# Thresholded attention and a GELU layer pair on one core: moving the weights' conversion within the first batch, and zeroing less of the V tiles

## The chip, the cores and the metric

The kernel runs on one core of one Trainium2 chip. The metric is the device time of one execution in microseconds (us); the median of several runs is compared. Five engines work side by side, each through its own instructions in order, and wait for one another by semaphores: TensorE (PE; its weight loads are shown apart as PEld), VectorE (DVE), ScalarE (ACT), GpSimd (POOL) and SyncE (SP, which here only issues transfers).

## The reference

```python
scores = scale * q @ k.T                       # per batch and head, S x S
thresh = max(scores, axis=-1) - tau
scores = where(scores >= thresh, scores, -1e9)
attn = exp(scores - max(scores)); attn = attn / (sum(attn) + 1e-9)
x = (attn @ v)  ->  (B*S, H*D)                 # 4608 x 512
h = x @ w_in                                   # 512 x 2048
g = 0.5 * h * (1 + erf(h / sqrt(2)))
out = g @ w_out                                # 2048 x 512
```

There are 8 batches, 8 heads, 576 tokens and a head size of 64. Queries, keys and values are 32-bit floats. The two weight matrices come as 64-bit floats, because a 32-bit array was multiplied by a 64-bit scalar when they were made. The kernel turns each weight into a 32-bit float by integer arithmetic on its two halves. This is the conversion that the change moves.

## The kernel before

**Pairs, chunks and slots.** Heads are handled in pairs (`p`, 32 pairs, 4 to a batch, `HP = 4`). The 576 query rows of a pair are cut into five chunks: four of 128 rows for both heads (`i` = 0 to 3) and one (`i` = 4, `NC`) that holds the 64 last rows of both heads. The main loop (L1065) goes over slots `n`, one pair and one chunk each. In the first batch (`BATCH` = 20 slots) the order is special: first chunks 0 and 1 of all four pairs (n = 0 to 7), then chunks 2, 3 and 4 of each pair in turn (n = 8 to 19). So n = 10, 13, 16 and 19 are the short chunks.

**One slot.** `scores` (L403) puts the products of a chunk into two PSUM tiles `sc`, one for each head of the pair. There are just two such buffers, so the scores of the next slot wait until the last reader of these is done. `softmax_head` takes the row maximum on VectorE (L415), the threshold on GpSimd (L416) and the exponential on ScalarE (L418). `softmax_tail` zeroes what lies under the threshold and sums the rows, in one VectorE instruction for each head (L435), which is that last reader. In the first batch, TensorE turns the result in the slot after (`turn_p_early`, L349), with copies on ScalarE (L356, L365); `weigh_v` multiplies it with the values (L538), and `divide_early` (L457 to L465) divides by the sums. For the first slots of the first pairs, queries and keys are turned on TensorE too (`turn_qk_early`, L319 to L336).

**The first layer beside the attention.** When 256 tokens have all their heads, a block of the two matrix layers can start. `fill` (L638) puts products of the first layer (L614) and of the second (L629) between the attention's products, by a budget of time that the list `GOAL` sets. In the first batch it starts at slot 10 and does the first half of block 0; a product is placed only when its weight pieces have been converted.

**Conversion of the weights.** There are 32 pieces of 128x512 weights, 16 of each matrix, 512 KB each as 64-bit floats. `load_piece` (L183) brings a piece into a free place of `xall` or `turned_p`. `conversions` (L186) is a generator that issues the steps of one piece after another: two ScalarE instructions (L202 for the high half's power, L203 for the low half), two VectorE instructions on the piece before (L210, L212), then the load of another piece. `add_low_bits` (L222) adds the two parts on GpSimd (L226) in a later slot. `convert(ns)` is called at the end of every slot. It adds `ns` to a debt and takes steps until the VectorE time that they stand for, 340 + 720 = 1060 ns a piece, has paid it. All engines work through their instructions in order, so what `convert` puts at the end of a slot stands before the maximum, the exponential and the later work of the next slot.

**The V tiles.** Four tiles `v_sb` of 128 x 2 x 5 x 64 hold the values of a pair. For the first four pairs, `load_v_early` fills chunks 0 to 3 of both heads in all partitions, and of the last chunk (index `NC` = 4) only 64 partitions for each head; the other 64 must be zero, because the short chunks of both heads are multiplied in one go. The tiles are zeroed once at the start, on VectorE, before the first scores (L1027, L1028).

Of the kernel before, what the change touches and what calls it, by code (L numbers as in the profile page):

```python
# [18 lines left out]
def kernel(  # L19
# [35 lines left out]
    HP = H // 2  # L55
    NP = B * HP
    EARLY = HP
    NC = S // P
# [66 lines left out]
    q_tail = [att.tile([P, P], FP32, name=f"q_tail{i}") for i in range(4)]  # L125
    v_sb = [att.tile([P, 2, KR, D], FP32, name=f"v{i}") for i in range(4)]
# [59 lines left out]
    def conversions():  # L186

        vec = nc.vector
        ahead = []
        done = 0
        while raws or ahead:
            if raws:
                dst, raw, slot = raws.pop(0)
                lo, hi = (raw.rearrange("p (f w) -> p f w", w=2)[:, :, i] for i in range(2))  # L200
                power = gp.tile([P, PIECE], U32, tag="g", name="power")
                nc.scalar.activation(power.bitcast(FP32), hi.bitcast(FP32), AF.Copy, bias=0.0, scale=2.0 ** -112)  # L202
                nc.scalar.activation(dst.bitcast(U32), lo, AF.Copy, bias=0.0, scale=2.0 ** -29)  # L203
                ahead.append((dst, hi, power, slot))
                yield 0
            if len(ahead) == LATER and done == len(pieces) - LATER:
                yield None
            if len(ahead) == 2 or not raws:
                dst, hi, power, slot = ahead.pop(0)
                vec.tensor_scalar(power, power, 3, 0x7FFFFFF8, op0=ALU.logical_shift_left, op1=ALU.bitwise_and)  # L210
                yield 340
                vec.scalar_tensor_tensor(power, hi, 0x80000000, power, op0=ALU.bitwise_and, op1=ALU.bitwise_or)  # L212
                x_free.extend(slot)
                yield 720
                sums_due.append((dst.bitcast(U32), power))
                load_piece()
                done += 1
                yield 0
# [3 lines left out]
    def add_low_bits(most=len(pieces)):  # L222

        for _ in range(min(most, len(sums_due))):
            dst, power = sums_due.pop(0)
            nc.gpsimd.tensor_tensor(dst, power, dst, op=ALU.add)  # L226
            converted[0] += 1
# [3 lines left out]
    def convert(ns, least=0):  # L231

        if conv["steps"] is None:
            conv["steps"] = conversions()
        conv["debt"] += ns
        while conv["debt"] > 0 or least > 0:
            took = next(conv["steps"], None)
            if took is None:
                return
            conv["debt"] -= took  # L240
            least -= took
# [31 lines left out]
    def load_early(p):  # L273
        b, hp = divmod(p, HP)
        s = st[p] = {}
        for name, src in (("q", q), ("k", k)):

            if p == 2:
                at = s[name + "_slot"] = x_slot()
                t = x_rows(at)[:, 0:2 * (NC + 1) * D].rearrange("p (e c d) -> p e c d", e=2, d=D)  # L280
            else:
                t = ld.tile([P, 2, NC + 1, D], FP32, tag=name, name=name)
            s[name] = t
            eng = (nc.scalar, nc.gpsimd)[p] if p < 2 and name == "k" else nc.sync
            for e in range(2):
                rows = src[b, 2 * hp + e, 0:MAIN, :]
                if name == "q":
                    eng.dma_start(t[:, e, 0:NC, :].rearrange("p (g c) d -> p g (c d)", c=2),
                                  rows.rearrange("(g p c) d -> p g (c d)", p=P, c=2))
                else:  # L290
                    eng.dma_start(t[:, e, 0:NC, :], rows.rearrange("(p t) d -> p t d", p=P))
            eng.dma_start(t[0:TAIL, :, NC, :], src[b, 2 * hp:2 * hp + 2, MAIN:S, :].rearrange("e s d -> s e d"))
# [101 lines left out]
    def scores(p, i):  # L394
        s = st[p]
        n = 1 if i == NC else 2
        sc = s["sc", i] = [ps.tile([P, 2, 512], FP32, tag="sc", name="sc", bufs=2) for _ in range(n)]
        for h in range(2):
            for e in range(n):
                rows = slice(0, P) if i == NC else slice(e * D, (e + 1) * D)  # L400
                lhsT = s["q_tail"] if i == NC else s["qT"][rows, i * P:(i + 1) * P]
                at = h * HALF + (TAIL if p < EARLY and e == 0 else 0)
                nc.tensor.matmul(  # L403
                    sc[e][:, h, 0:HALF], lhsT=lhsT, rhs=s["kT"][rows, at:at + HALF], start=True, stop=True)
# [36 lines left out]
    def invert(p, i):  # L441

        den = st[p]["sum", i]
        nc.vector.reciprocal(den, den)
# [579 lines left out]
    for _ in range(2):  # L1024
        load_piece(nc.gpsimd)
    load_early(2)
    for t in q_tail + v_sb:  # L1027
        nc.vector.memset(t, 0.0)  # L1028
    turn_qk_early(0)
    conv["steps"] = conversions()  # L1030
# [10 lines left out]
    BATCH = HP * SLOTS  # L1041
# [23 lines left out]
    for n in range(len(slots) + WEIGH + 1):  # L1065
        p, i = slots[n] if n < len(slots) else divmod(n, SLOTS)
        early = p < EARLY
        last = slots[n - 1] if 0 < n <= len(slots) else None
        if p < NP:
            scores(p, i)  # L1070
            softmax_head(p, i)
            add_low_bits()
            if last and last[0] < EARLY:
                invert(*last)
            if p < HP - 1 and i == 0:
                turn_qk_early(p + 1)
        elif n == len(slots):
            early_end.close()
            weights_first()
        gelus(0)  # L1080
        if n == BATCH:
            gelus_held()
        table()
        for args in due:
            weigh_v(*args)
            divide_early(*args)
        due = []
        if p > EARLY and i == WEIGH:
            for lo, hi in (0, WIDE), (WIDE, S):
                weigh_v(p - 1, lo, hi)  # L1090
            if p == NP:
                divide(p - 1)
        owed += (goal(n) - goal(n - 1)) * BLK_NS * (PARTS[i] if not early and p < NP else 1.0)
        if early:
            fill(owed, tokens)
            owed = 0.0
            table()
        if last and last[0] < EARLY and last[1] < NC:
            turn_p_early(*last)
        if p < NP:  # L1100
            softmax_tail(p, i)
        if p < NP and not early:
            turn_p(p, i)
        if p < NP and not early:
            if i == 2:
                regroup(p, 1)
            if i > 2:
                regroup(p, i)
            if i == NC:
                divisors(p)  # L1110
        if last and last[0] < EARLY and last[1] == NC:
            turn_p_early(*last)
        if p < 2 and i == 0:
            for _ in range(2):
                load_piece()
            load_v_early(p + 2)
        if p == 1 and i == NC:
            load(HP)
        if n == BATCH - 3:
            load(HP + 1)  # L1120
        if n == BATCH:
            for t in pd_tail + [turned_p[:, e, h, :, :] for e in range(2) for h in range(2)]:
                nc.gpsimd.memset(t[:, NB:4 * KR, :], 0.0)
        if EARLY < p < NP and i == DIVIDE:
            divide(p - 1)
        if p >= HP and i == 1 and p + 2 < NP:
            loads = load_steps(p + 2)
        if p >= HP:
            next(loads, None)
        if p >= HP and i == 1 and p + 1 < NP or p == HP - 1 and i == 2:  # L1130
            scale_q(p + 1)
        if p >= HP - 1 and i == 2 and p + 1 < NP:
            turn_qk(p + 1)
        convert(0 if n == 0 else 1200 if n < 3 else 1900 if n < BATCH - 1 else 1e9)
        if not early:
            lag[0] = 2 if p < NP else 0
            if n != BATCH:
                fill(owed, tokens)
                owed = 0.0
        if last and last[0] < EARLY:  # L1140
            if last[1] == 1:
                due.append((last[0], 0, TOK))
            if last[1] == NC:
                due.append((last[0], TOK, S))
        if n == START - 1:
            tokens = TOK
        elif n == BATCH + 1:
            tokens = S
        elif p > EARLY and i == DIVIDE and p % HP == 0 or p == NP and i == WEIGH:
            tokens = p // HP * S  # L1150
            leaving += [n for n in AWAY if n in x_blk and (n + 1) * TOK <= tokens]
        elif leaving and i < 2:
            put_away(leaving.pop(0))
# [35 lines left out]
```

## Time and profile before

| what | value |
|---|---|
| median of 3 runs | 1350.75 us (1350.1 to 1352.02) |
| profiled span | 1351.2 us, 19824 instructions |
| busy: TensorE, VectorE, ScalarE, GpSimd | 98%, 77%, 45%, 49% |
| granted TensorE clock, mean | 0.989 |
| slot 0, slot 10, slot 18 open (first row maximum) | 11.32, 70.88, 124.27 us |
| zeroing of the four V tiles | 2.61 us of VectorE, from 6.12 |
| L210, L212 (VectorE, one piece) | 0.42 and 0.69 us, when nothing is in the way |
| L226 (GpSimd, one piece) | 1.26 us |

The profile is that of one execution. A group line names source line, engine, operation and tiles; the bracket at the end gives the idle time of the engine just before, and what ended it ("<-DVE p L435": VectorE's instruction of line 435 that wrote p; "issue": nothing that the profile shows). The clock column is the share of the full TensorE clock that was granted in a stretch. A busy TensorE is not a TensorE at its peak: the ends of matmuls are modelled, and a stretch at half clock is as busy as one at full clock.

### The profile page before, as it was taken

The page shows a single profiled execution, that of the slowest core. Times are in us where ns is not written, and L with a number is a line of the kernel's source. Part 1 is how long each engine was busy: PE and PEld are TensorE (multiplying, and loading weights), DVE is VectorE, ACT ScalarE, POOL GpSimd, SP SyncE. Part 2 cuts the span into 40 slices and gives each one's busy share as a digit, 9 for nine tenths or more (in the row PEclk, how much of TensorE's full clock was granted, in tenths as well). Part 3 has the DMA queues.
Part 4 walks back from the last instruction along what each step waited for, and adds up shares of the span by engine and source line. Part 5 has one row for each costly group of instructions (what it writes and reads, how often), then busy time and mean ns, then how long its engine had stood idle before and what let it go on. Part 6 is the DMA issues. An engine that isn't in the chain of part 4 may idle for free.

```text
span 1351.2 us, 19824 instructions
## 1 busy us (share of the span) xinstructions
PE 1326.1 (98%) x6282; PEld 895.3 (66%) x6282; DVE 1043.9 (77%) x2005; ACT 605.6 (45%) x1027; POOL 657.2 (49%) x1091
## 2 busy tenths in 40 slices
PE   8899899999999999999999999999999999999998
PEld 6577457467467467457557557568787787877877
DVE  6877687788888888878888888874758698385775
ACT  7877437438447538437638536413201112211120
POOL 4766444555655565554554551144363513635530
PEclk8899899999999999999999999999999999999999
DMA  8743276677778687787688677500000031000003
GB/s 258 188 137 76 67 168 147 149 169 182 159 179 176 159 202 168 162 207 167 153 210 181 150 180 150 117 8 0 1 0 1 16 110 32 0 1 0 1 0 78
DMA packets 209782, 152.40 MB, mean 113 GB/s; under 512 B 113360, under 2 KB 193088, under 8 KB 209680
## 3 DMA queue, kind: packets, MB, share of 16 engines
q1 hardware_dynamic: 187648, 110.43, 37.1%
q0 software_dynamic: 21312, 39.37, 10.5%
q10 hardware_dynamic: 720, 1.34, 0.3%
q8 instruction: 51, 0.84, 0.3%
q14 instruction: 51, 0.42, 0.1%
HBM read 55.97 MB, written 12.52 MB: 51 GB/s over the span
## 4 chain that ended last, share of the span: by engine, by line
PE 93%; ACT 2%; DMA 2%; DVE 1%; issue 1%; POOL 0%; SPq 0%; DVEq 0%; ACTq 0%; POOLq 0%
PE bank L802 34%; PE o_ps L629 17%; PE hT L614 16%; PE sc L403 14%; PE xT L538 11%; DMA x<-xall 1%; DMA q<-in_q_dram 1%; ACT p L418 1%; PE tr L349 1%; DVE nmx L415 1%; ACT pT L356 0%; DVE p L435 0%; PE tr L457 0%; ACT power L202 0%; DVE power L212 0%
## 5 line engine op out<-in xcount | busy, mean ns | idle before, releaser
L418 ACT ACTIVATE p<-sc,nmx 128x576 f32<-128x576 f32 x288 | 201.9, 739 | 278.7 <-DVE nmx L415 278.5
L435 DVE SCALAR_TENSOR_TENSOR p<-sc,thr,p 128x576 f32<-128x576 f32 x288 | 226.2, 816 | 77.9 <-ACT p L418 71.4
L416 POOL TENSOR_SCALAR thr<-nmx,tau_eff 128x1 f32<-128x1 f32 x288 | 85.3, 296 | 369.0 <-DVE nmx L415 359.4
L415 DVE TENSOR_REDUCE nmx<-sc 128x1 f32<-128x576 f32 x288 | 205.4, 750 | 53.4 <-PE sc L403 52.1
L614 PE MATMUL hT<-xall,w_in 128*128 128x256 f32 x1024 | 243.0, 387 | 0.0
L629 PE MATMUL o_ps<-w_out,g 128*128 128x512 f32 x512 | 238.4, 606 | 0.0
L614 PEld LDWEIGHTS hT<-xall,w_in 128*128 128x128 f32 x1024 | 190.4, 191 | 50.5 <-issue 23.0
L684 DVE TENSOR_TENSOR c<-c,bank 128x320 f32<-128x320 f32 x304 | 147.2, 488 | 33.7 <-PE bank L802 20.5
L684 DVE TENSOR_TENSOR o<-o,bank 128x256 f32<-128x256 f32 x240 | 99.8, 420 | 93.7 <-PE bank L802 88.7
L403 PE MATMUL sc<-kT,qT 64*128 64x288 f32 x960 | 161.8, 434 | 9.8 <-DVE p L435 9.1
L538 PE MATMUL xT<-pT,v 128*64 128x256 f32 (+1 forms) x1280 | 168.0, 416 | 0.1
L629 PEld LDWEIGHTS o_ps<-w_out,g 128*128 128x128 f32 x512 | 93.7, 191 | 110.2 <-issue 107.6
L499 DVE STREAM_TRANSPOSE turned_p<-p 128x1152 f32<-128x1152 f32 x112 | 154.4, 1378 | 3.9
L403 PEld LDWEIGHTS sc<-kT,qT 64*128 64x128 f32 x960 | 92.2, 188 | 83.4 <-issue 69.5
L538 PEld LDWEIGHTS xT<-pT,v 128*64 128x64 f32 x1280 | 91.4, 140 | 75.3 <-issue 14.6
L802 PE MATMUL bank<-w_out,c 128*128 128x256 f32 x480 | 120.2, 381 | 0.5 <-DVE o L684 0.5
L269 POOL DMA_DIRECT2D v<-in_v_dram x208 | 111.3, 538 | 3.7 <-issue 1.3
L802 PEld LDWEIGHTS bank<-w_out,c 128*128 128x128 f32 x480 | 89.9, 190 | 18.8 <-DVE o L684 3.0
L855 ACT ACTIVATE c<-c 128x320 f32<-128x320 f32 (+1 forms) x80 | 46.9, 623 | 114.6 <-DVE c L684 114.5
L684 POOL TENSOR_TENSOR c<-c,g 128x320 f32<-128x320 f32 (+1 forms) x40 | 50.6, 1273 | 67.4 <-DVE c L684 67.4
L802 PE MATMUL bank<-t_out,c 128*128 128x256 f32 x320 | 82.7, 381 | 0.0
L802 PE MATMUL bank<-t_out,g 128*128 128x256 f32 x320 | 82.1, 379 | 0.0
(179 smaller groups left out, 1771.8 us busy)
## 6 DMA issues: line engine op xcount, KB each, us to landing
pT<-turned_p SPq DMA_DIRECT2D x448, 160.0 KB, 3.6
pT<-pd_tail SPq DMA_DIRECT2D x112, 80.0 KB, 3.0
q<-in_q_dram POOLq DMA_DIRECT2D x104, 72.0 KB, 3.8
k<-in_k_dram POOLq DMA_DIRECT2D x104, 72.0 KB, 3.2
inv<-turned SPq DMA_DIRECT2D x54, 128.0 KB, 4.0
v<-in_v_dram POOLq DMA_DIRECT2D x156, 40.0 KB, 3.1
out_dram<-o SPq DMA_DIRECT2D x40, 128.0 KB, 2.4
xall<-in_moe_w_out_dram POOLq DMA_DIRECT2D x9, 512.0 KB, 4.4
```

The lines of the kernel that those rows point to most:

```text
L269: eng.dma_start(t[r:P:4, e, 0:n, :], rows[:, r * KR:r * KR + n, :])
L403: nc.tensor.matmul(sc[e][:, h, 0:HALF], lhsT=lhsT, rhs=s["kT"][rows, at:at + HALF], start=True, stop=True)
L415: nc.vector.tensor_reduce(nmx[:, e:e + 1], sc, axis=AXIS.XY, op=ALU.max, negate=True)
L416: nc.gpsimd.tensor_scalar(thr[:, e:e + 1], nmx[:, e:e + 1], -1.0, tau_eff, op0=ALU.mult, op1=ALU.subtract)
L418: nc.scalar.activation(w[:, e * S:(e + 1) * S].rearrange("p (h s) -> p h s", h=2), sc, AF.Exp, bias=nmx[:, e:e + 1], scale=1.0)
L435: nc.vector.scalar_tensor_tensor(row, sc[e][:, :, 0:HALF], thr[:, e:e + 1], row, op0=ALU.is_ge, op1=ALU.mult, accum_out=den[e])
L499: nc.vector.transpose(turned_p[:, :, i // 2, 0:NB, i % 2 * Q:(i % 2 + 1) * Q], w.rearrange("p (e b i) -> p e b i", e=2, i=Q))
L538: nc.tensor.matmul(to, lhsT=s["v"][:, e, c, :], rhs=rhs, start=(c == 0), stop=(c == KR - 1))
L614: nc.tensor.matmul(hT[:, j % 2, :], lhsT=w_in_sb[c][:, j * P:(j + 1) * P], rhs=x_blk[n][:, c, :], start=(c == 0), stop=(c == N_DM - 1))
L629: nc.tensor.matmul(o[:, 0:d_model], lhsT=g[j][:, m * P:(m + 1) * P], rhs=w_out_sb[j], start=(j == 0), stop=(j == N_DF - 1))
L684: eng.tensor_tensor(out, a, b, op=ALU.add)
L802: nc.tensor.matmul(to, lhsT=l, rhs=r, start=start and k == 0, stop=k == len(pairs) - 1, skip_group_check=not start)
```

## The change

It has two parts. The first spreads the conversion differently over the first batch. Before, every slot from 3 to 18 adds 1900 ns to the debt. After, slots 3 to 8 add 1000 ns and slots 9 to 18 add 2450 ns. The total is nearly the same (32,800 and 32,900 ns with the slots before), so that all weights are still ready at the end of the batch. It is for the slots in which TensorE has little to do beside the attention: in slots 3 to 8 the other engines then have less beside the softmax, and more of the conversion comes where TensorE has products of the first layer to do.

The second zeroes only the chunk with index `NC` of each V tile, 128 instead of 640 columns, since chunks 0 to 3 are overwritten by the loads. It is for VectorE's work before the first slot.

```diff
@@ -1024,7 +1024,7 @@
     for _ in range(2):
         load_piece(nc.gpsimd)
     load_early(2)
-    for t in q_tail + v_sb:
+    for t in q_tail + [t[:, :, NC, :] for t in v_sb]:
         nc.vector.memset(t, 0.0)
     turn_qk_early(0)
     conv["steps"] = conversions()
@@ -1131,7 +1131,7 @@
             scale_q(p + 1)
         if p >= HP - 1 and i == 2 and p + 1 < NP:
             turn_qk(p + 1)
-        convert(0 if n == 0 else 1200 if n < 3 else 1900 if n < BATCH - 1 else 1e9)
+        convert(0 if n == 0 else 1200 if n < 3 else 1000 if n < 2 * HP + 1 else 2450 if n < BATCH - 1 else 1e9)
         if not early:
             lag[0] = 2 if p < NP else 0
             if n != BATCH:
```

Counted by the ScalarE instructions L202 between the exponentials of one slot and of the next, the 32 pieces fall on the slots like this:

| slot n | start | 0 | 1 | 2 | 3 | 4 | 5 | 6 | 7 | 8 | 9 | 10 | 11 | 12 | 13 | 14 | 15 | 16 | 17 | 18 |
|---|---|---|---|---|---|---|---|---|---|---|---|---|---|---|---|---|---|---|---|---|
| before | 1 | 0 | 2 | 1 | 2 | 1 | 2 | 2 | 2 | 2 | 1 | 2 | 2 | 2 | 1 | 2 | 2 | 2 | 2 | 1 |
| after | 1 | 0 | 2 | 1 | 1 | 1 | 1 | 1 | 0 | 1 | 3 | 2 | 2 | 3 | 2 | 2 | 3 | 2 | 2 | 2 |

## The prediction

> **What bounds the kernel now.** I read the page first (parts 1, 2 and 4), then busy time by stage, then the first 142 us in order of time.
>
> ```profile
> PE 1326.1 (98%) x6282; PEld 895.3 (66%) x6282; DVE 1043.9 (77%) x2005; ACT 605.6 (45%) x1027; POOL 657.2 (49%) x1091
> ...
> PE   8899899999999999999999999999999999999998
> ...
> PE 93%; ACT 2%; DMA 2%; DVE 1%; issue 1%; POOL 0%; SPq 0%; DVEq 0%; ACTq 0%; POOLq 0%
> ```
>
> TensorE sets the time, and its work and order are the same in both kernels: laid side by side, all matmuls of the changed program stand in the old order. So only TensorE's idle time and its clock can change. Both are at the start, as busy time by stretch shows (after the stretch come its length, then busy us and count of PE, PEld, DVE, ACT, POOL; then clock, DMA share, GB/s):
>
> ```profile
> 26.86:70.88 44.02, 37.77 (x268) 26.01 (x269) 36.37 (x74) 36.66 (x75) 32.65 (x50) 0.84 0.70 194
> 70.88:124.27 53.39, 50.86 (x300) 37.87 (x300) 39.81 (x80) 41.16 (x84) 34.53 (x52) 1.00 0.45 127
> 124.27:141.81 17.54, 14.89 (x87) 10.95 (x85) 13.39 (x29) 12.82 (x25) 10.31 (x20) 0.94 0.06 13
> 141.81:1351.20 1209.39, 1200.39 (x5456) 803.63 (x5452) 938.38 (x1781) 497.64 (x809) 567.59 (x943) 1.00 0.48 108
> ```
>
> I number slots n by the row maximum (L415) that opens them: n=3 opens at 26.86, n=10 at 70.88, n=18 at 124.27. In n=3 to 9 TensorE idles 6.25 us and runs at 0.84 of its clock; in n=10 to 17 it idles 2.5 us at full clock; after 141.81 it is busy 99%. Time won or lost before 141.81 should reach the end.
>
> The clock, in stretches of 3.41 us laid on the instants at which it changes:
>
> ```profile
> 16.67:20.08 3.41, 1.88 (x12) 1.18 (x11) 3.23 (x9) 3.21 (x7) 0.94 (x3) 1.00 0.94 324
> 20.08:23.50 3.42, 3.42 (x28) 2.67 (x27) 2.92 (x8) 3.33 (x6) 2.44 (x4) 0.50 0.93 245
> ...
> 33.73:37.15 3.42, 2.46 (x25) 1.78 (x23) 2.93 (x7) 3.38 (x9) 3.30 (x5) 1.00 1.09 291
> 37.15:40.56 3.41, 3.32 (x30) 1.95 (x27) 2.70 (x7) 3.36 (x8) 2.49 (x4) 1.00 1.30 209
> ...
> 43.97:47.39 3.42, 0.67 (x7) 0.44 (x5) 3.12 (x7) 3.24 (x7) 2.00 (x4) 1.00 0.87 248
> 47.39:50.80 3.41, 3.39 (x10) 1.72 (x10) 3.12 (x6) 2.98 (x7) 2.75 (x5) 0.50 0.23 78
> 50.80:54.21 3.41, 3.41 (x17) 1.91 (x18) 2.93 (x7) 1.41 (x2) 2.57 (x5) 0.50 0.91 265
> ```
>
> A stretch in which PE was busy 1.88 us or less is followed by half clock; one with 2.46 us is not. The two pauses that cost most end at 47.39 and 61.04 (1.07 us busy before that); each is followed by two stretches at 0.50. The wait that ends them:
>
> ```profile
> 47.38 0.50 PEld L403 LDWEIGHTS sc<-pd_tail,qT 64*128 64x128 f32 x2 [2.98 <-issue]
> 47.41 3.42 PE L403 MATMUL sc<-pd_tail,qT 64*128 64x288 f32 x8 [2.77 <-DVE p L435]
> ```
>
> The next scores wait for the last read of the old ones (L435), which waits for the exponential (L418), which stands on ScalarE behind conversions (L202, L203). ScalarE is busy 17.35 of 17.95 us from 26.86 to 44.81.
>
> **What the Trainium skill says.** "TensorE: Matmul & The Clock Gate", Part 1, has a free-running window of 3413 ns, half clock after an idle one and full clock after a busy one. The trace agrees on the window (drops at 20.08, 47.39 and 61.04 lie 8 and 4 windows apart), but drops after half-idle windows too. "SBUF — State Buffer", Who interferes with whom: a VectorE instruction with two SBUF inputs, or in a two-port mode, and a GpSimd instruction that reads SBUF exclude each other. The trace agrees: L212 takes 0.69 us alone, 1.65 at 114.64 beside GpSimd adds (L226). "VectorE: DVE Perf Modes", Zero memsets: a cycle per element; the four 128x640 zeroings took 2.61 us, 0.65 each, as that says.
>
> **The change, part by part.**
>
> *Zeroing.* Four zeroings of 640 columns (2.61 us) become four of 128. Four of 128x128 (q_tail) took 0.59, so VectorE is free 2.0 us earlier. Its next instruction, the copy of kT (L324), ended at 9.28; but the scores it feeds also need ScalarE's L333, which ended at 9.22 and waited for a transfer of q. Worth 0.06 us.
>
> *Conversion moved.* One piece costs ScalarE about 1.15 us start to start (L202, L203), VectorE 0.42 + 0.69 = 1.11 (L210, L212), GpSimd 1.26 (L226). Counted in the two programs' orders on ScalarE, slots 3 to 8 lose 1, 0, 1, 1, 2, 1 pieces: six. Gained: slot 9 two, slots 12, 13, 15 and 18 one each. All weights are still converted before the first block's products use them.
>
> *What slots 3 to 9 give.* Carrying the removed pieces through the waits:
> - n=4: its exponential waited until 33.84 behind two pieces; with one it starts 1.1 us earlier.
> - n=5 keeps this 1.1. n=6: one piece fewer on both engines, maxima and exponential 2.45 us earlier.
> - The scores at 47.41 then start near 44.85. At full clock they end about 47.0, against 50.83.
> - n=7: two pieces fewer, and its values (L538, 20 rows) take 2.5 us at full clock (26.76 shows 2.52) instead of 4.06: n=8 opens about 5.7 earlier.
> - n=8, n=9: the same once more (L538 at 64.08 took 4.23). The scores of n=10 come at about 61.1 instead of 69.71.
>
> So 8.6 us if neither pause drops the clock. A pause of some 2.1 us remains in slot 6 and of 1.5 us in slot 8, and by the stretches above 1.0 to 1.5 us of idleness in one window can be enough. One window at half clock costs 3.41/2 = 1.7 us. I take half of one: 7.7 us; the bounds are 8.6 and 8.6 - 2 x 1.7 = 5.2.
>
> *What the later slots take back.* VectorE and ScalarE have 12 to 13 us to spare in n=10 to 17, so by the sums 5 or 6 pieces fit. But much of this spare time is waiting in line: at 91.19, L210 had waited 2.50 us for a ScalarE result that stands behind copies of TensorE's transposes. And this chain is tight:
>
> ```profile
> 96.77 1.42 DVE L415 TENSOR_REDUCE nmx<-sc 128x1 f32<-128x576 f32 x2
> ...
> 99.58 0.82 DVE L435 SCALAR_TENSOR_TENSOR p<-sc,thr,p 128x576 f32<-128x576 f32 x1 [0.35 <-POOL thr L416]
> 99.72 0.29 PEld L403 LDWEIGHTS sc<-pd_tail,qT 64*128 64x128 f32 x2 [0.17 <-PE tr L349]
> ```
>
> - Slot 9, two pieces: the maximum of n=10 comes 2 us later against TensorE, under 3.2 us of first-layer products (70.68). What waits is its L435 and then the scores of n=11 and 12: 0.7 to 1.5 us.
> - Slots 12 and 13, two pieces: the exponential of n=13 is 1.2 us later (behind a third piece on ScalarE), and 1.1 us of L210 and L212 stand before the maximum of n=14. The scores of n=15 wait for all: 2.3 us. If conversions fill the gaps that GpSimd's adds left in L212 (94.32 took 1.47), 1.1.
> - Slot 15, one piece: in the same way 0.7 to 1.55 us at the scores of n=18.
> - Slot 18, one piece: 0 to 0.7 us at the scores of n=21.
>
> Sum 2.5 to 6.05 us; I take the middle, 4.3. Transfers of weights move with their pieces; the DMA share is 0.45 in n=10 to 17, so they stay hidden, and the early share of 0.70 falls.
>
> Sum: 1350.75 - 0.06 - 7.7 + 4.3 = 1347.3.
>
> **The rivals.**
> - *Given back in full.* The chain before n=15 and n=18 has no slack and the clock drops again: gain 8.6 less two half-clock windows (3.4) = 5.2, give-back 6.05: 1351.6, no change. For it: the tight chain above, and idleness of some 2 us that would stand before the scores of n=15. Against it: the spare time by sums.
> - *Slower.* The same with half clock once or twice more, after longer pauses before the scores of n=15 and n=18 (1.7 each), and adds and L212 excluding each other (0.8 more): 1353.3 to 1355.8. For it: TensorE is busy 95% there, so every pause is new. Against it: slot 9 takes two pieces almost for nothing.
> - *Moved at no cost.* The second stage hides all but 1.6 us, the clock stays full: 1350.75 - 8.6 + 1.6 = 1343.8. For it: 2.5 us of idle time on TensorE there. Against: the in-order queues.
>
> **How the numbers follow.** The forecast and the rival below it, counting only what ends under 1348.05, have 0.52 (0.40 and 0.12); the first rival with the forecast's slow edge has 0.25; the slower one 0.23. The range reaches from 1342.5 (rival three, 1343.8, with the drop at 139.55 also gone by luck of the window) to 1353.5 (the start of the slower case), leaving about 0.1 on each side.
>
> **What would show it right or wrong.** Right: the scores of n=10 at about 61 to 63 instead of 69.71, at most one half-clock window between 40 and 65, ScalarE no longer 97% busy up to n=6, and pauses of 1 to 3 us before the scores of n=15 and n=18 that were under 1 us. Wrong: two windows of 0.50 again after slots 6 and 8 (the early gain is then under 5.2), or new windows of 0.50 in n=14 to 18 (the late loss is then over 6). After the first batch, stretches of equal length should match within 1 us; if not, the time went where I don't look.

## The result, and the profile after

| | before | after |
|---|---|---|
| median | 1351.12 us (1350.1 to 1352.43, 6 runs) | 1361.66 us (1359.67 to 1362.61, 6 runs) |
| ratio, 95% interval | | 1.0075 (1.0062 to 1.0088): slower by 0.75% |
| profiled span, mean clock | 1351.2 us, 0.989 | 1360.2 us, 0.989 |

The change costs 10.5 us where the forecast had a gain of 3.5. The first lines of the page of the kernel after look almost as before (parts 1 and 2; a digit is a tenth, and a slice is 34 us):

```profile
PE 1329.1 (98%) x6282; PEld 893.8 (66%) x6282; DVE 1044.6 (77%) x2005; ACT 605.0 (44%) x1027; POOL 656.0 (48%) x1091
...
PE   8888899999999999999999999999999999999998
```

TensorE is 3 us longer busy with as many instructions, and two of its early slices that read 9 now read 8. The busy time by stage shows where TensorE runs slower and waits more. The stages are those of the prediction, cut at the row maxima of n = 3, 10, 18 and 21; after the length come busy us and count of PE, PEld, DVE, ACT and POOL, then clock, DMA share and GB/s:

```profile
24.34:65.60 41.26, 37.36 (x277) 25.89 (x278) 30.28 (x65) 32.62 (x68) 24.42 (x41) 0.92 0.55 141
65.60:131.28 65.68, 55.59 (x286) 38.75 (x286) 47.32 (x90) 44.82 (x91) 43.18 (x61) 0.90 0.48 149
131.28:150.70 19.42, 15.84 (x95) 11.54 (x93) 14.56 (x30) 13.91 (x27) 11.72 (x21) 0.94 0.04 10
150.70:1360.20 1209.50, 1200.34 (x5456) 803.48 (x5452) 938.33 (x1781) 497.33 (x810) 565.87 (x943) 1.00 0.48 108
```

- The early slots (n = 3 to 9) became 2.8 us shorter (44.02 to 41.26). With what the kernel was ahead at n = 3 (24.34 against 26.86), n = 10 opens 5.3 us earlier. The 2.5 us at n = 3 aren't due to the moved conversion, which begins in that slot: with the old schedule n = 3 opens at 24.54 us in experiment 1 and at 24.56 in experiment 3.
- n = 10 to 17 became 12.3 us longer (53.39 to 65.68). TensorE idles 10.1 us there instead of 2.5, and its clock falls from 1.00 to 0.90. 0.10 of 65.68 us is 6.6 us, near four windows at half clock (4 x 1.7). That is TensorE's own time; how much of it reaches the end of the stage is not told by this sum.
- n = 18 to 20 lost 1.9 us (17.54 to 19.42).
- After the first batch the stretches agree within 0.11 us (1209.50 and 1209.39). The whole loss is in the first 151 us.

The opening times say more closely where the advance goes. It is 6.7 us at n = 9, 5.3 at n = 10, 4.3 at n = 12, -0.2 at n = 13, -4.4 at n = 16, -7.0 at n = 18 and -8.9 at n = 21. The largest step, 4.4 us, is slot 12; slots 13, 15 and 16 lose about 2 us each, while slots 11 and 14 lose nothing. So the loss comes in the short slots (n = 10, 13, 16) and in the slots two after them (n = 12, 15, 18).

The chain of waits of the kernel after shows what sets the time there. This is part of its answer for 64 to 84 us, in order of time (start, us, what):

```profile
66.95 0.64 ACT p L418
...
68.50 1.37 DVE power L212
69.87 1.43 DVE power L210
...
72.39 0.69 DVE power L212
73.08 0.68 DVE nmx L415
...
74.25 1.23 POOL w_in L226
75.48 0.28 POOL thr L416
...
76.77 2.25 PE sc L403 x6
79.02 5.06 PE xT L538 x19
```

The same view of the kernel before, for its slots 10 to 12:

```profile
70.85 3.02 PE hT L614 x14
...
75.59 0.58 ACT power L202
...
76.19 0.44 DVE power L210
...
76.65 0.69 DVE power L212
77.34 0.68 DVE nmx L415
```

In the kernel before, TensorE's products carry the chain until it passes through one L210 and one L212 at their free durations, 0.44 and 0.69 us. After, it runs through three pieces on ScalarE (L202 and L203, 63.52 to 66.95), the exponential of the short chunk, a whole queue of conversions on VectorE, and only then the maximum of n = 11. And the first two of VectorE's take 1.37 and 1.43 us. (One add of about 1.2 us stands before the second threshold L416 in both chains, at 74.25 and at 78.52, so that is no difference between the kernels.) Why, the timeline of the kernel after shows (start, us, engine, line, tiles; the bracket is the idle time before):

```profile
66.82 4.18 POOL L226 TENSOR_TENSOR w_in<-power,w_in 128x512 uint32<-128x512 uint32 x3
...
68.42 1.45 DVE L212 SCALAR_TENSOR_TENSOR power<-xall,power 128x512 uint32<-128x512 uint32 x1
...
69.79 1.50 DVE L210 TENSOR_SCALAR power<-power 128x512 uint32<-128x512 uint32 x1
...
71.93 0.42 DVE L210 TENSOR_SCALAR power<-power 128x512 uint32<-128x512 uint32 x1
...
75.59 0.72 PE L403 MATMUL sc<-kT,qT 64*128 64x288 f32 x2 [2.41 <-DVE p L435]
```

Three adds stand back to back on GpSimd from 66.82 to 71.00 (one add a piece, and three pieces had fallen due). While they run, L212 and L210 take 1.45 and 1.50 us; the L210 at 71.93, after the last of them, takes 0.42. The next scores then make TensorE wait 2.41 us, and the clock follows. These are stretches of 3.41 us of the kernel after:

```profile
73.25:76.67 3.42, 0.72 (x2) 0.29 (x2) 2.93 (x8) 2.83 (x7) 2.73 (x4) 1.00 0.82 293
76.67:80.08 3.41, 3.31 (x12) 1.74 (x14) 3.34 (x6) 2.19 (x5) 1.92 (x5) 0.50 0.34 82
80.08:83.49 3.41, 3.41 (x16) 1.63 (x14) 0.39 (x2) 1.57 (x3) 2.88 (x4) 0.50 0.58 228
```

One pause, two windows at half clock: this is why the values (L538) at 79.02 take 5.06 us, against 2.84 in the kernel before. The same pattern comes again before n = 15 (a pause of 2.21 us, L212 at 1.48 and L210 at 1.50), and the long L212 and L210 come a third time in n = 16 (1.43 and 1.50). In the kernel before, one L212 is held in n = 13 and in n = 16 too (1.47 and 1.65), but there only one or two adds come in a row, and no L210 of n = 10 to 20 takes over 0.75 us.

### The profile page after: what moved, and what is told of

The parts are those of the page before. It is cut to its first block, busy times and chain, and to the rows that moved or that the text cites. A ratio compares the mean times of both kernels' runs of the same rounds, so it can differ in the third digit from the quotient of the medians.

```text
span 1360.2 us, 19830 instructions
## 1 busy us (share of the span) xinstructions
PE 1329.1 (98%) x6282; PEld 893.8 (66%) x6282; DVE 1044.6 (77%) x2005; ACT 605.0 (44%) x1027; POOL 656.0 (48%) x1091
## 4 chain that ended last, share of the span: by engine, by line
PE 92%; DMA 2%; DVE 2%; ACT 2%; issue 1%; POOL 1%; SPq 0%; DVEq 0%; ACTq 0%; POOLq 0%
PE bank L802 33%; PE o_ps L629 17%; PE hT L614 15%; PE sc L403 13%; PE xT L538 12%; DMA xall<-in_q_dram 1%; DMA x<-xall 1%; ACT p L418 1%; DMA v<-in_v_dram 1%; PE tr L349 1%; DVE power L212 1%; DVE power L210 1%; DVE nmx L415 0%; ACT power L202 0%; DVE p L435 0%
## 5 line engine op out<-in xcount | busy, mean ns | idle before, releaser
L435 DVE SCALAR_TENSOR_TENSOR p<-sc,thr,p 128x576 f32<-128x576 f32 x288 | 226.0, 816 | 85.4 <-ACT p L418 72.6
L416 POOL TENSOR_SCALAR thr<-nmx,tau_eff 128x1 f32<-128x1 f32 x288 | 84.5, 293 | 366.5 <-DVE nmx L415 357.6
L614 PE MATMUL hT<-xall,w_in 128*128 128x256 f32 x1024 | 242.7, 386 | 0.0
L614 PEld LDWEIGHTS hT<-xall,w_in 128*128 128x128 f32 x1024 | 190.1, 190 | 50.4 <-issue 23.0
L538 PE MATMUL xT<-pT,v 128*64 128x256 f32 (+1 forms) x1280 | 172.2, 423 | 0.1
L538 PEld LDWEIGHTS xT<-pT,v 128*64 128x64 f32 x1280 | 92.3, 142 | 79.0 <-issue 20.4
```

The lines of the kernel that those rows point to most:

```text
L416: nc.gpsimd.tensor_scalar(thr[:, e:e + 1], nmx[:, e:e + 1], -1.0, tau_eff, op0=ALU.mult, op1=ALU.subtract)
L435: nc.vector.scalar_tensor_tensor(row, sc[e][:, :, 0:HALF], thr[:, e:e + 1], row, op0=ALU.is_ge, op1=ALU.mult, accum_out=den[e])
L538: nc.tensor.matmul(to, lhsT=s["v"][:, e, c, :], rhs=rhs, start=(c == 0), stop=(c == KR - 1))
L614: nc.tensor.matmul(hT[:, j % 2, :], lhsT=w_in_sb[c][:, j * P:(j + 1) * P], rhs=x_blk[n][:, c, :], start=(c == 0), stop=(c == N_DM - 1))
```

## The experiments

The theory is: VectorE's conversion steps and GpSimd's adds shut each other out, and the change put both on the chain that leads from a short chunk to the next scores. Rivals: the moved VectorE and ScalarE work is too much by itself; GpSimd's queue is occupied; a ring of buffers is full; the clock alone does it. All ratios are to the kernel before in the same session, and in brackets stands the 95% interval.

**1. The zeroing alone.** The kernel before with only the smaller zeroing:

```diff
-    for t in q_tail + v_sb:
+    for t in q_tail + [t[:, :, NC, :] for t in v_sb]:
```

> The kernel before with only the smaller zeroing. If the loss comes from the conversion alone, this is 0 to 1 us faster than before (1350 to 1351); slot 0 opens up to 0.9 us earlier. If the start takes part in the loss, it is slower by a part of the 10.5 us.

Measured: 1350.88 us, 0.9998 (0.9984 to 1.0012). The zeroing makes no difference that can be measured, which leaves it about 2 us either way; the loss of 10.5 us is due to the conversion.

**2. The changed kernel without GpSimd's adds.**

```diff
             dst, power = sums_due.pop(0)
-            nc.gpsimd.tensor_tensor(dst, power, dst, op=ALU.add)
             converted[0] += 1
```

> The changed kernel without GpSimd's additions (L226): the two parts of the weights are not added, so the products use the low part alone. If the exclusion between these additions and L210/L212 is a main cause: L210 goes back from 0.64 to 0.43 us on average and L212 to 0.70, and the time falls by 4 to 8 us (1353.5 to 1357.5). If it is not: within 2 us of 1361.7.

Measured: 1346.96 us, 0.9969 (0.9957 to 0.998). That is some 14 us faster than with the adds, more than the 4 to 8 expected. n = 10 to 17 take 54.45 us instead of 65.68, at clock 1.00. The schedule that lost 10.5 us to the kernel before is faster than it when the adds are gone. So the moved work of VectorE and ScalarE is not too much by itself.

**3. The kernel before without the adds** (the same edit in the kernel before).

> The kernel before without GpSimd's additions (L226), the control for the changed kernel without them: the weights' high part is not added, so the products use the low part alone. If the exclusion between additions and L210/L212 hits the moved conversion above all, this gains 0 to 4 us (1346 to 1350) and the changed kernel without additions is as fast or faster. If the additions cost both kernels alike, this gains 10 or more and the difference of 10 us between the two remains.

Measured: 1348.62 us, 0.9981 (0.9974 to 0.9989). So the adds cost the kernel before 0.19% (2.6 us) and the changed one 1.0075 less 0.9969, or 1.06% (14 us). Without adds the change itself is worth 0.12%, 1.7 us; the two intervals overlap, so this gain is not clear of the noise. Between these two kernels n = 10 opens 6.0 us earlier (63.44 and 69.44), n = 10 to 17 take 2.8 us more (54.45 and 51.64) and n = 18 to 20 0.4 more (17.27 and 16.88).

**4. Fills in place of the adds.** The adds occupy GpSimd and read SBUF. Two fills of the same tile occupy it nearly as long and read nothing:

```diff
-            nc.gpsimd.tensor_tensor(dst, power, dst, op=ALU.add)
+            for _ in range(2):
+                nc.gpsimd.memset(power.bitcast(FP32), 0.0)
```

> The changed kernel with each GpSimd add L226 (1.26 us, two inputs read from SBUF) replaced by two fills of the tile power (128x512 each, which read nothing; from the 128x256 fill of 0.31 us, L264, about 0.55 us each, so 1.1 us), in the same place and order. The low bits are not added: the product takes part of each weight. It tells whether the adds harm because GpSimd's queue is occupied (threshold, sums and products stand behind them) or because they shut VectorE out of SBUF. Exclusion theory: L210 and L212 of n = 10 to 20 at their free times (0.45 and 0.69 to 0.75 us), n = 10 to 17 in 53.5 to 56 us, total 1346 to 1349 us, as without adds (1346.96). Queue theory: GpSimd is as long occupied as with adds, n = 10 to 17 in 62 to 66 us, total 1358 to 1362.

Measured: 1345.51 us (1344.44 to 1346.32), 0.9954 (0.9938 to 0.9971), a little under the window of the exclusion theory and far from that of the queue. A fill took 0.533 us, two of them 1.07 where an add takes 1.26. The groups of VectorE's conversion steps from n = 10 to 20 (count, busy us, mean ns, idle before), first of the changed kernel:

```profile
L210 DVE TENSOR_SCALAR power<-power 128x512 uint32<-128x512 uint32 x22 | 14.2, 644 | 6.1 <-ACT power L202 6.1
L212 DVE SCALAR_TENSOR_TENSOR power<-xall,power 128x512 uint32<-128x512 uint32 x12 | 9.8, 817 | 0.3
L212 DVE SCALAR_TENSOR_TENSOR power<-turned_p,power 128x512 uint32<-128x512 uint32 x10 | 8.1, 814 | 0.3
```

then with fills:

```profile
L210 DVE TENSOR_SCALAR power<-power 128x512 uint32<-128x512 uint32 x22 | 10.8, 491 | 5.8 <-ACT power L202 5.8
L212 DVE SCALAR_TENSOR_TENSOR power<-xall,power 128x512 uint32<-128x512 uint32 x12 | 8.3, 692 | 0.3
L212 DVE SCALAR_TENSOR_TENSOR power<-turned_p,power 128x512 uint32<-128x512 uint32 x10 | 7.3, 733 | 0.3
```

and the stages of the kernel with fills, n = 3 to 9 and n = 10 to 17:

```profile
23.71:61.03 37.32, 33.95 (x277) 24.16 (x278) 30.70 (x66) 32.56 (x68) 22.94 (x47) 1.00 0.61 158
61.03:116.30 55.27, 50.70 (x304) 37.39 (x304) 42.23 (x89) 44.64 (x91) 38.20 (x80) 1.00 0.59 178
```

With GpSimd busy 38.20 us of that stage, the steps run at nearly their free durations and n = 10 to 17 take 55.27 us. So the loss does not come from GpSimd's being occupied. What the fills lack is the reading of SBUF. They also take away a wait that a product of the first layer could have had for its added weights; but in the changed kernel no product (L614) waited for an add between 60 and 151 us, and the only instruction that did was one copy on ScalarE, for 0.3 us. The Trainium skill ("SBUF — State Buffer", Who interferes with whom) says just this: a VectorE instruction with two SBUF inputs contends with a GpSimd instruction that reads SBUF, not with one that only writes it. L212 agrees (817 ns and 814 beside adds, 692 and 733 beside fills). L210 has one input, so this sentence doesn't cover it; the runs show it held by the adds as well (644 ns in the mean, 491 beside fills).

The groups also show that the loss is not the sum of these durations. That sum falls by 5.7 us (32.1 to 26.4) over n = 10 to 20, while n = 10 to 17 alone become 10.4 us shorter. The rest follows from the chain: pauses of TensorE, and half clock after them. The next experiment was meant to part these two.

**5. Added products before the scores.** The changed kernel with eight products of the identity before the scores of slots i = 3 of the first batch (n = 9, 12, 15 and 18), meant to keep the clock up through the pause:

```diff
+        if p < EARLY and i == 3:
+            keep = ps.tile([P, NC, P], FP32, tag="mm", name="keep")
+            for k in range(8):
+                nc.tensor.matmul(keep[:, k % NC, :], lhsT=ident, rhs=ident, start=True, stop=True)
```

> The changed kernel, with eight matmul rows of the identity (1.7 us, read by nobody) before the scores of slots 9, 12, 15 and 18, where TensorE pauses. If half clock after these pauses is a third or more of the loss: the windows of 0.50 after slots 12, 15 and 18 go, 3 to 6 us faster than the changed kernel (1355.5 to 1358.5). If it is the pauses alone: within 1 us of it, or slower.

Measured: 1359.48 us (1354.33 to 1361.56), 1.0068 (1.0044 to 1.0091). By its total it can't be told from the changed kernel, and lies between the two windows expected. The profiled run took 1354.33 us, the fastest of the five by 4.7 us. In it n = 10 to 17 take 62.75 us at clock 1.00, 2.9 less than in the changed kernel and 7.5 more than with fills. This doesn't part the clock from the delay, because the added products stand in the way themselves (in this kernel L401 is the added product, L407 the scores, L439 the last reader):

```profile
73.28 2.05 PE L401 MATMUL keep<-ident 128*128 128x128 f32 x16 [2.62 <-ACT pT L360]
...
75.26 1.24 PE L407 MATMUL sc<-kT,qT 64*128 64x288 f32 x8
```

TensorE still pauses for 2.62 us before them, until ScalarE's copy L360 sets a PSUM tile free for them. They take 2.05 us, not the 1.7 expected, and the scores follow only at 75.26, though the last reader had ended at 74.12. They stand before the scores in the same way at 97.05 and 121.38. So up to 6.15 us (3 x 2.05) of the 62.75 can be the experiment's own cost. Of the 10.4 us, between 1.3 and 7.5 are delay at full clock and between 2.9 and 9.1 the clock (an estimate from these figures). Which is larger stays open. The half clock comes after pauses, and these come with the adds: before n = 12 the pause is 2.41 us with adds and 0.76 with fills.

**6 and 7. Where the late pieces stand.** The changed kernel with the late share unevenly spread: 3750 ns in slots with n % 3 == 2 (run 6), or in those with n % 3 == 0 (run 7), 1900 ns in the other late slots:

```diff
-... else 2450 if n < BATCH - 1 else 1e9)
+... else (3750 if n % 3 == 2 else 1900) if n < BATCH - 1 else 1e9)
```

> The changed kernel, with the same early cut, but the six late pieces put at the end of slots 11, 14 and 17 (two more each) instead of spread. Theory A (the loss is the chain between the short chunks n = 10, 13, 16, 19 and the scores after next: pieces there cost, pieces before the value products of n = 12, 15, 18 do not): the early gain of 5 to 6.7 us is kept, 1344 to 1349. Theory B (the second half has no room for six more pieces, wherever they stand): 1357 or more.

> The changed kernel, with the same early cut, but the late pieces at the ends of slots 9, 12, 15 and 18, so right before the short chunks. Theory A (place decides): as slow as the changed kernel or slower, 1360 to 1368, at least 7 us above the placement at slots 11, 14 and 17. Theory B (sum decides): within 3 us of that placement, 1351 to 1356.

Measured: n % 3 == 2 gives 1353.18 us, 1.0019 (1.0006 to 1.0031); n % 3 == 0 gives 1359.93 us, 1.0073 (1.0044 to 1.0103). Run 6 lies between the windows of its two theories, so most of the loss goes, but the early gain is not kept. Run 7 is hardly more than a repeat of the changed kernel: counted as in the table of the change, it has four pieces in slot 9 instead of three and one in slot 18 instead of two, and is alike in the others; its total lies at the edge of theory A's window. So the comparison is between run 6 and the changed kernel's own spread. With the same early cut, the place of the extra pieces is worth 0.54%, some 7 us. What stands at the end of slots 9, 12 and 15 delays the exponential of a short chunk, and its adds run during that chunk. From slots 11 and 14 it falls into n = 12 and 15, which are long in the kernel before too (8.3 us from n = 12 to 13, against 5.2 from n = 13 to 14). In run 6, n = 10 to 17 take 55.83 us at full clock. It gives the rest back in n = 18 to 20 (22.75 us, clock 0.83): the extra pieces of slot 17 fall into n = 18, which takes 11.7 us in place of 6.6.

**8 and 9. No adds in short slots.** The changed kernel, and the kernel before, with the adds held back from the short slots of the first three pairs; they run in the slot after:

```diff
-            add_low_bits(1)
+            if i < NC or p >= HP - 1:
+                add_low_bits(1)
...
-            add_low_bits()
+            if i < NC or p >= HP - 1:
+                add_low_bits()
```

> The changed kernel, with no additions on GpSimd in the short slots n = 10, 13 and 16; they go into the slots after. If the back-to-back additions in these slots block L210 and L212 on the tight chain: L210 under 0.55 us on average, 4 to 8 us faster than the changed kernel (1353.5 to 1357.5). If what counts is only that the conversion stands there: within 2 us of 1361.7.

> The kernel before, with the additions of the short slots moved in the same way. It has at most two additions there, and one L212 of 1.47 and one of 1.65 us beside them: 0 to 2 us faster than before (1348 to 1350.5).

Measured: the changed kernel becomes 1354.18 us, 1.0033 (1.002 to 1.0045), 0.42% better than with the adds there and inside its window; the kernel before stays at 1350.86, 0.9992 (0.9983 to 1.0002), just above its window. The group of the changed kernel without adds in short slots:

```profile
L210 DVE TENSOR_SCALAR power<-power 128x512 uint32<-128x512 uint32 x22 | 15.0, 681 | 0.9 <-ACT power L202 0.9
```

The expected fall of L210 did not come. VectorE is shut out as long as before (681 ns mean against 644), only elsewhere: in slots in which the next scores don't wait for it. L212 takes 1.65, L210 1.50 and L212 1.64 us one after another in n = 11, and nearly the same in n = 14, yet no pause of over 0.6 us stands before the scores of n = 11 to 20. Over half of the loss went. So the sum of the time shut out is not what decides, but the place at which it stands.

**10. More buffers for the row sums.** In the changed kernel L435 waits three times, 4.0 us at most, for the division on TensorE (L457) that reads the sums of four slots earlier; before, it waited once, 0.9 us. (The expectation takes the longest of the three, 4.0 us, for their mean; together they are 7.0.)

```diff
-            pair = small.tile([P, 2], FP32, tag="den", name="den")
+            pair = small.tile([P, 2], FP32, tag="den", name="den", bufs=8)
```

> The changed kernel with 8 instead of 4 buffers for the tile of the row sums (den) of the early slots. In the changed kernel L435 of n = 12, 15 and 18 waits 4.0 us in the mean for the division L457 on TensorE that still reads the buffer of four slots before (before: once, 0.9 us). Theory that this wait is only a sign (TensorE is late and is itself what sets the time there): these waits go, total unchanged, 1359 to 1363. Rival (the ring of four sum tiles is what the later conversion runs into): pauses before n = 13, 16, 19 go, total 1352 to 1357.

Measured: 1359.6 us (1358.0 to 1361.77), 1.0058 (1.0041 to 1.0074). The three waits are gone, n = 10 to 17 take 65.64 us (65.68 without the buffers). The longest new wait on VectorE was a sign of TensorE being late, not a cause.

**11 and 12. Versions meant to beat both.** Both without adds in short slots, as in 8. Run 11 has a milder early cut, run 12 the whole one, with chosen slots for the late pieces:

```diff
+... else 1400 if n < 2 * HP + 1 else 3400 if n in (11, 14) else 1900 if n < BATCH - 1 else 1e9)
```

```diff
+... else 1000 if n < 2 * HP + 1 else 2800 if n == 2 * HP + 1 else 3750 if n in (11, 14) else 1900 if n < BATCH - 1 else 1e9)
```

> A milder change, with what the earlier runs say: 1400 ns in slots 3 to 8, 3400 ns in slots 11 and 14 alone (whose pieces stand before the slots in which TensorE has most other work), 1900 ns elsewhere, and no adds L226 in short slots before the last pair. Theory (what is taken back depends on where pieces and adds stand): early gain about 3 us, give-back 0 to 2: 1347 to 1350, ratio 0.997 to 0.9995. Rival (any conversion moved behind n = 9 costs more than it brings): 1351 to 1354.

> The whole early cut (1000 ns in slots 3 to 8), with 2800 ns in slot 9, 3750 ns in slots 11 and 14, 1900 ns elsewhere, and no adds L226 in short slots before the last pair. Theory (placement): early gain 5 to 7 us, give-back 3 to 6: 1346 to 1351. Rival: as the changed kernel without adds in short slots (1354.18), 1352 to 1356.

Measured: 1351.75 us, 0.9992 (0.9978 to 1.0005), and 1353.96 us, 1.0023 (1.0014 to 1.0032). The milder one ends level with the kernel before: by its ratio it is inside the theory's window, by its time inside the rival's, so it decides nothing. The other lies in the rival's window and is slower than the kernel before: the chosen places did not help beyond what experiment 8 had brought. No version that does all the work beat the kernel before by what can be measured; in each, what is moved out of the early slots is about given back.

## Why the prediction was wrong

**The step that failed** is "What the later slots take back": 4.3 us forecast with 2.5 to 6.05 as bounds. Counted where the prediction makes its cut, from the scores of n = 10, it is 16.0 us (7.1 ahead there, 62.57 against 69.71, and 8.9 behind at n = 21); from the row maximum of n = 10 it is 14.2. The mis-sized term is the duration of a late piece on VectorE where GpSimd has adds to do, and what follows from it: the pauses and the half clock. The step priced each L210 and L212 of the tight slots at the free 0.42 and 0.69 us (1.1 a piece), and put the exclusion into the "slower" rival, with 0.8 us for L212 alone. Three pieces before a short chunk mean three adds in a row during it, and beside those L212 took 1.45 and L210 1.50 us. Without the adds in both kernels the same count, from the scores of n = 10 to those of n = 21, gives 71.59 against 66.51 us, so 5.1 taken back (experiments 2 and 3, one profiled run each), inside the forecast's bounds. The kernel before had held the warning: the L212 of 1.65 us that the prediction itself quotes.

Point by point:

- *Only the first 142 us matter, and the rest of TensorE's work is as before.* Right: 1209.50 and 1209.39 us after the batch.
- *Zeroing worth 0.06 us.* In keeping with experiment 1, whose interval is wider than that. But the wait was misread: in the changed kernel the first scores start at 8.99 us, before ScalarE's L333 ends at 9.54; only the later ones of them wait for it, 0.30 us. In the three traces with the larger zeroing (before, experiments 3 and 9) they start 0.14 or 0.15 us after the copy of kT has ended (9.42, 9.65 and 10.20), and slot 0 opens at 10.90 to 12.49. In those with the smaller one the copy ends by 8.68, and slot 0 opens at 9.51 to 10.91. The smaller zeroing may well open slot 0 earlier, by up to about 1 us; that this reaches the end is not shown.
- *Early gain 7.7 us, bounds 5.2 to 8.6.* Too high as well: from the scores of n = 3 to those of n = 10 the gain is 4.6 us (39.50 against 44.12), and the rest of the 7.1 came before n = 3. The mechanism was right: the two pauses before scores shrank from 2.77 and 2.44 us to 2.32 (in two parts, 1.52 and 0.80) and 1.51, near the 2.1 and 1.5 forecast. The half-clock term was mis-sized: half of one window was assumed, two came (clock 0.92 over 41.26 us, 3.3 us lost). Which windows drop may depend on how the pauses lie to them; no run steered that. Among the experiments whose slots 3 to 8 are those of the changed kernel, stage n = 3 to 9 took from 37.00 us (experiment 10, clock 1.00) to 42.89 (experiment 8, clock 0.88). In experiment 10 the gain counted by the scores is 8.9 us (35.24 against 44.12), near the forecast's 8.6 at full clock.
- *Pauses of 1 to 3 us before the scores of n = 15 and n = 18.* Right as far as it goes: 2.21 us before n = 15, and 2.24 just before the scores of n = 18 (there ended by ScalarE's copy of a first-layer product, L581, not by L435). But 2.41 us came before n = 12 too, which the step had put at 0.7 to 1.5 us for the two pieces of slot 9.
- *Half clock in the later slots.* The sum left it out; the "slower" rival had it once or twice more, and the signs of being wrong named it. It came in four windows of n = 10 to 17. Both of those signs came true: one window of 0.50 after the pause of slot 6 and one after that of slot 8, with an early gain under 5.2 us, and new windows in n = 14 and n = 17 (at 103.97 and 127.88), with a late loss over 6.
- *Transfers stay hidden.* Nothing speaks against it: the DMA share of n = 10 to 17 is 0.48 (0.45 before), and no wait for weights stands in the chain shown.

The "slower" rival had the right side and the right parts (pauses, clock, exclusion), each too small: it ended at 1355.8 us, and the kernel came to 1361.66. It was given 0.23: against it stood that slot 9 takes two pieces almost for nothing, and against the rival that it builds on, the spare time by sums. In the changed kernel slot 9's three pieces stand before the longest of these pauses (2.41 us). The sums were sound for VectorE and ScalarE as long as no adds ran (n = 10 to 17 then hide the moved work with 2.8 us lost, 54.45 against 51.64), but they took each instruction's duration as its own, not as a matter of its neighbour's.

What stays open: how the loss divides into delay and half clock, since experiment 5 doesn't part them; and why some pauses end in half clock and others don't. The kernel before was not run with fills, so for the fills there is no such control as experiment 3 is for the missing adds.

## What to carry to other kernels

Before work is moved next to other work, look in the trace for the longest single execution of each instruction involved, not the mean: if it is two or three times the shortest, a neighbour may be shutting it out, and the move may put the two side by side on a chain that has no slack. Judge a slot for spare work by what waits for its end, not by its sum of busy times; here the place of the same pieces was worth 7 us. An experiment that replaces a suspect by one that occupies its engine as long, but lacks the suspected property (fills for adds), tells a queue from a conflict in one run. A filler that is meant to keep an engine busy through a wait can itself delay what waits (experiment 5), so look in its trace at what it stands in front of.

## What the runs showed of the hardware

- VectorE's in-place integer instruction with one input (L210) was held longest of all in proportion: 0.42 us free, 1.50 beside GpSimd adds. Beside fills it was 491 ns in the mean, against 450 with GpSimd free of both: writing alone held it little.
- Three adds in a row on GpSimd took 4.18 us, the longest single one 1.72 us against 1.26 alone, while VectorE's two instructions beside them took two to four times as long (0.69 to 1.45, 0.42 to 1.50). The three adds lost 0.4 us together, the two VectorE instructions 1.8.
- In the changed kernel, windows with TensorE busy for 0.72 us (73.25) and 1.85 us (100.56 to 103.97) were followed by half clock; in the Trainium skill ("TensorE: Matmul & The Clock Gate", Part 1) the slow state comes after an idle window. Here a half-idle one can be enough. But the busy time alone doesn't decide, and the line that the prediction drew at 1.88 us doesn't hold in other runs: in experiment 8 a window with 1.56 us (82.48 to 85.89) was followed by full clock, in experiment 12 one with 2.33 us (15.66 to 19.07) by half.
